# Half of one input load issued from GpSimd's queue instead of SP's

## Chip, cores and metric

The kernel runs on one core of a Trainium2 chip. The metric is the device time of one execution in microseconds (us); before the change it is 413.87 us, the median of 3 runs (413.44 to 415.31).

## What is computed

The input x has 2048 tokens of 448 features. A gate mixes two branches. Branch a is attention with 16 heads of 28 features, in which each token looks at itself and 7 earlier tokens, 2 apart. Branch b is an MLP with 1792 hidden features, biases and a squared ReLU. Cut to what matters:

```
g = sigmoid((x * gate_w).sum(-1, keepdims=True))
q, k, v = split(x @ wqkv)                      # 448 -> 3 x 448
idx = pos[:, None] - 2 * arange(8)             # masked where negative
a = softmax_w(q . k[idx] * 28 ** -0.5) . v[idx] @ wo
b = square(relu(x @ w1 + b1)) @ w2 + b2
out = g * a + (1 - g) * b
```

## The kernel before

**Numbers.** All matrix products keep nearly full float32 accuracy by splitting. Each operand is held as a rounded part (h, for high) and a rest (l, for low), and each product is three matmuls: h by h, h by l, l by h. ScalarE makes the high part by a copy into the rounded type, VectorE the low part by a subtraction.

**Tiles.** The 2048 tokens are cut into four row tiles of 512 tokens (`CH`), numbered c = 0 to 3. The 448 features, over which the first products sum, are cut into K tiles of 128, 128, 128 and 64 rows (k = 0 to 3). The host hands x over transposed, as `xT[c, row, k, token]`, and the weights as `wqkv[b, row, k, column]` with b = 0, 1, 2 for q, k and v.

**Stages.** First the q, k and v products of the four row tiles, beginning with row tile 0 in `qkv_first` (L246); then the MLP on TensorE (`h_first`, `o_part` and so on), beside which GpSimd and VectorE compute the attention (L329 to L346), and at the end the output projection with `wo`. The order of the instructions is written out by hand: `advance` (L471) adds up costs of the matmuls issued so far and emits the other engines' steps when they fall due. Each engine works through its own instructions in the order in which the program emits them.

**The start, where the change is.** Before any data is there, TensorE runs 13 matmuls on zeros (L625). The loads for row tile 0 are issued in the loop at L630, all from SP: for each k the q weights of K tile k (L632, 225 KB; for k = 3 in two parts, L635), and then K tile k of row tile 0 into `rx` (L637), whose name in the profile is xraw. For k = 0 this second load comes in two halves of 256 tokens, 128 KB each; for k = 1 to 3 it is one load of 256 KB. Behind them SP issues the loads of the weights of k and v (L642, L645) and of row tile 1 (`x_load`, L558).

The splits follow in the loop at L647, for k = 0, 1, 2: ScalarE rounds the weights (L648, `wqh`), then the two halves of x (L655), except that the very first half is rounded by VectorE (L653); VectorE subtracts (L656 for the weights, L658 for the halves of x). The last K tile is split at L659 and L660 through `split_full` (L114).

`qkv_first` then takes the K tiles in order. For each k it computes tokens 0 to 255 (output tiles 0 and 1) and then tokens 256 to 511 (output tiles 2 and 3), six matmuls each, at L255:

```
for k in range(3):
    for two in ((0, 1), (2, 3)):
        for j, prods in enumerate(zip(*(full(x, q[i], i, 0, (k,)) for i in two))):
            for acc, a, w in prods:
                nc.tensor.matmul(acc.pt[:, :D], a, w, start=k == j == 0, stop=False)
```

So the second half of K tile 0 is needed by the seventh matmul, and K tile 1 by the thirteenth. The last 64 rows of K, and all of k and v, follow through `side_by_side` (L178, matmul at L186).

GpSimd's instructions up to there are memsets: four constants of the launch, `mask` (L106, L108) and `halo0` (L162). Its next work in program order is the first attention product (L331). Before the change it issues no DMA.

Of the kernel before, what the change touches and what calls it, by code (L numbers as in the profile page):

```python
# [22 lines left out]
CH = 512  # L23
# [34 lines left out]
def gated_mix_kernel(ctx: ExitStack, tc: tile.TileContext, xT, wqkv, w1, w2, wo, b1, b2, out):  # L58
    nc = tc.nc
# [432 lines left out]
    def raw_tile(name):  # L492
        return rawp.tile([P, 4, 512], F32, tag="raw", name=name)
# [135 lines left out]
    rx = raw_tile("xraw0")  # L629
    for k in range(4):  # L630
        if k < 3:
            nc.sync.dma_start(raws[0][:, k, :NQ], wqkv[0, :, k])  # L632
        else:
            for b, rows in ((0, slice(0, 64)), (1, slice(64, P))):
                nc.sync.dma_start(raws[0][rows, k, :NQ], wqkv[b, rows, k])  # L635
        for cols in ((slice(0, 256), slice(256, CH)) if k == 0 else (slice(0, CH),)):
            nc.sync.dma_start(rx[:, k, cols], xT[0, :, k, cols])  # L637

    for b, tag in ((1, "k"), (2, "v")):
        raw = attp.tile([P, 3, D], F32, tag=tag, name=f"wqraw{b}")  # L640
# [569 lines left out]
```

## Time and profile before

| | |
|---|---|
| median of 3 runs | 413.87 us (413.44 to 415.31) |
| profiled execution, its own time | 413.75 us |
| its span (first to last instruction) | 412.0 us |
| DVE (VectorE) busy | 270.5 us, 66% |
| ACT (ScalarE) busy | 210.5 us, 51% |
| POOL (GpSimd) busy | 268.5 us, 65% |
| granted TensorE clock | 1.0 |
| DMA through SP's queue | 73.23 MB; none from another engine's queue |

PE is TensorE, PEld its weight loads, which overlap the matmuls; SPq is SP's queue of DMA issues and POOLq the steps of GpSimd's queue that count as no busy time. A row of the timeline gives start, duration, engine, line, operation, the tiles written and read, their shapes, how many instructions are merged, and in brackets the idle time of the engine ahead of it and what ended it. A row of the waits gives the total in us, how often, and the longest. In the view by stretches each engine has its busy time with the number of its instructions, in the order PE, PEld, DVE, ACT, POOL; behind them stand the granted clock, the busy share of the 16 DMA engines, and GB/s.

### The profile page before, as it was taken

What the parts mean: (1) busy time and instruction counts of PE and PEld (TensorE: products, weight loads), DVE (VectorE), ACT (ScalarE), POOL (GpSimd) and SP (SyncE); (2) the same over time, 40 slices, a digit from 0 to 9 for tenths busy, and PEclk for the clock granted to TensorE, in tenths of its full rate; (3) what the DMA queues carried; (4) which work ended last, traced back from release to release, by engine and by line L of the source; (5) the groups of instructions that cost most, each with busy time, mean ns of one, the idle gap of its engine ahead of it and who ended that gap; (6) DMA issues with size and microseconds to landing.
All of it is one profiled execution on the core that took longest, in us unless ns stands there. A gap on an engine that the chain in (4) does not pass through costs nothing.

```text
span 412.0 us, 9325 instructions
## 1 busy us (share of the span) xinstructions
PE 407.2 (99%) x3835; PEld 371.7 (90%) x3835; DVE 270.5 (66%) x430; ACT 210.5 (51%) x461; POOL 268.5 (65%) x167
## 2 busy tenths in 40 slices
PE   8999999999999999999999999999999999999996
PEld 7999999999999999888888888988898888888996
DVE  4690845287767766787656798879576677882354
ACT  4642647387765555444565535444653254356640
POOL 0000000966989999989989899999899977940000
PEclk9999999999999999999999999999999999999999
DMA  7999899988272325554103649765146530168304
GB/s 215 378 343 324 246 373 277 366 276 302 91 258 82 128 64 196 209 185 152 50 38 113 215 157 270 196 163 141 31 151 196 220 130 2 45 166 147 93 0 181
DMA packets 66331, 73.83 MB, mean 179 GB/s; under 512 B 33072, under 2 KB 59248, under 8 KB 65904
## 3 DMA queue, kind: packets, MB, share of 16 engines
q1 hardware_dynamic: 66288, 73.23, 55.4%
q8 instruction: 30, 0.49, 0.5%
q14 instruction: 13, 0.11, 0.1%
HBM read 45.74 MB, written 28.28 MB: 180 GB/s over the span
## 4 chain that ended last, share of the span: by engine, by line
PE 97%; DMA 1%; SPq 0%; DVE 0%; ACT 0%; issue 0%
PE b L186 33%; PE h L186 32%; PE qkv L186 23%; PE a L186 7%; PE qkv L255 1%; DMA xraw<-xT 1%; PE a L984 1%; PE last L984 0%; SPq L637 0%; SPq L632 0%; DVE bt L863 0%; ACT x L655 0%; PE last L976 0%; PE a L976 0%
## 5 line engine op out<-in xcount | busy, mean ns | idle before, releaser
L331 POOL TENSOR_TENSOR qk<-q,k 128x896 f32<-128x896 f32 x64 | 135.2, 2148 | 83.8 <-DMA k<-k_d 77.1
L338 POOL TENSOR_TENSOR av<-lg,v 128x896 f32<-128x896 f32 x64 | 119.4, 1965 | 6.3 <-DVE lg L332 5.8
L612 DVE TENSOR_TENSOR h<-h,h 128x512 fp32r<-128x512 f32 x56 | 38.4, 688 | 66.3 <-ACT h L615 66.0
L186 PE MATMUL qkv<-wqh,x 64*128 64x448 f32 x528 | 78.6, 359 | 0.0
L186 PE MATMUL b<-w2ah,h 64*128 64x448 f32 x448 | 67.2, 359 | 0.0
L332 DVE TENSOR_REDUCE lg<-qk 128x32 f32<-128x896 f32 x64 | 66.9, 1074 | 0.0
L186 PE MATMUL b<-w2bh,h 64*128 64x448 f32 x448 | 66.8, 360 | 0.0
L346 DVE TENSOR_REDUCE o<-av 128x112 f32<-128x896 f32 x64 | 66.4, 1070 | 0.1
L613 ACT ACTIVATE h<-h,b1z 128x512 f32<-128x512 f32 x56 | 36.7, 655 | 43.6 <-PE h L186 43.6
L186 PEld LDWEIGHTS qkv<-wqh,x 64*128 64x128 f32 x528 | 50.7, 184 | 2.7
L186 PE MATMUL qkv<-wql,x 64*128 64x448 f32 x264 | 48.8, 359 | 0.0
L186 PEld LDWEIGHTS b<-w2bh,h 64*128 64x128 f32 x448 | 42.8, 184 | 3.3 <-ACT h L564 0.3
L186 PEld LDWEIGHTS b<-w2ah,h 64*128 64x128 f32 x448 | 43.1, 184 | 2.9
L186 PE MATMUL b<-w2al,h 64*128 64x448 f32 x224 | 41.2, 358 | 0.0
L186 PE MATMUL b<-w2bl,h 64*128 64x448 f32 x224 | 41.1, 358 | 0.0
L205 ACT ACTIVATE st<-qkv 128x448 f32<-128x448 f32 x48 | 23.4, 540 | 32.5 <-PE qkv L186 28.6
L614 ACT ACTIVATE h<-h 128x512 fp32r<-128x512 f32 x56 | 33.5, 598 | 1.7
L615 ACT ACTIVATE h<-h 128x512 f32<-128x512 f32 x56 | 33.3, 594 | 0.0
L186 PE MATMUL h<-x,w1h 64*128 64x512 f32 x168 | 29.6, 386 | 0.0
L564 ACT ACTIVATE h<-h 128x4 fp32r<-128x4 f32 (+1 forms) x35 | 7.2, 207 | 43.6 <-PE b L186 43.4
L186 PE MATMUL h<-x0b,w1h 64*128 64x512 f32 x168 | 28.1, 386 | 0.0
L186 PE MATMUL h<-x1b,w1h 64*128 64x512 f32 x168 | 28.1, 386 | 0.0
(150 smaller groups left out, 694.2 us busy)
## 6 DMA issues: line engine op xcount, KB each, us to landing
k<-k_d SPq DMA_DIRECT2D x8, 840.0 KB, 5.5
v<-v_d SPq DMA_DIRECT2D x8, 840.0 KB, 4.5
x_d<-x SPq DMA_DIRECT2D x11, 512.0 KB, 7.3
q_d<-st SPq DMA_DIRECT2D x8, 448.0 KB, 5.6
k_d<-st SPq DMA_DIRECT2D x8, 448.0 KB, 6.6
v_d<-st SPq DMA_DIRECT2D x8, 448.0 KB, 6.5
w1raw<-w SPq DMA_DIRECT2D x4, 896.0 KB, 9.8
q<-q_d SPq DMA_DIRECT2D x8, 448.0 KB, 3.7
```

What stands on the lines that cost most here:

```text
L186: nc.tensor.matmul(acc.pt[:, :acc.n], a[rows], w[rows], start=acc.todo == acc.all, stop=acc.todo == 1)
L205: nc.scalar.activation(st[:, :, t % 2], pt[:, :D].rearrange("p (g c) -> p g c", g=G), AF.Copy)
L255: nc.tensor.matmul(acc.pt[:, :D], a, w, start=k == j == 0, stop=False)
L331: nc.gpsimd.tensor_mul(pr, q[:, s:s + 1].to_broadcast([P, W, C]), k[:, s:s + W])
L332: pending.append(lambda: nc.vector.tensor_reduce(lg[:, s], pr.rearrange("p w (h d) -> p w h d", h=HG), axis=AX.X, op=ALU.add))
L338: nc.gpsimd.tensor_mul(pr.rearrange("p (h d) w -> p w h d", h=HG), lg[:, s][:, :, :, None].to_broadcast([P, W, HG, DH]), v[:, s:s + W].rea ...
L346: nc.vector.tensor_reduce(o[:, g * C:(g + 1) * C], pr, axis=AX.X, op=ALU.add)
L564: nc.scalar.activation(ap, f32(ap), AF.Copy)
L612: nc.vector.tensor_sub(hl, pt, f32(hh))
L613: ops += [lambda pt=pt, r=r: nc.scalar.activation(pt, pt, AF.Relu, bias=b1t[:, f + r:f + r + 1]), lambda pt=pt, hh=hh: nc.scalar.activatio ...
L614: lambda pt=pt, hh=hh: nc.scalar.activation(hh, pt, AF.Square),
L615: lambda pt=pt, r=r, low=low: (nc.scalar.activation(pt, pt, AF.Square), at(delays[r], low))]
```

## The change

The load of tokens 256 to 511 of K tile 0 of row tile 0 is issued by GpSimd instead of SP. Its place in the program, its source, its destination and its size are the same, and so are all other loads; for k = 1 to 3 the code is only written differently.

```
         else:
             for b, rows in ((0, slice(0, 64)), (1, slice(64, P))):
                 nc.sync.dma_start(raws[0][rows, k, :NQ], wqkv[b, rows, k])
-        for cols in ((slice(0, 256), slice(256, CH)) if k == 0 else (slice(0, CH),)):
-            nc.sync.dma_start(rx[:, k, cols], xT[0, :, k, cols])
+        if k == 0:
+            nc.sync.dma_start(rx[:, 0, 0:256], xT[0, :, 0, 0:256])
+            nc.gpsimd.dma_start(rx[:, 0, 256:CH], xT[0, :, 0, 256:CH])
+        else:
+            nc.sync.dma_start(rx[:, k], xT[0, :, k])
```

## The prediction

> **What bounds the kernel now.** I read the page's busy table and its chain first, to learn which engine sets the end, and then the chain in order of time for the first 14 us, because the moved transfer is issued there.
>
> ```profile
> PE 407.2 (99%) x3835; PEld 371.7 (90%) x3835; DVE 270.5 (66%) x430; ACT 210.5 (51%) x461; POOL 268.5 (65%) x167
> ...
> 1.66 0.43 SPq L637
> 2.09 0.04 issue
> 2.13 0.43 SPq L632
> 2.56 0.04 issue
> 2.60 4.56 DMA xraw<-xT
> 7.16 0.02 issue
> 7.18 0.43 ACT x L655
> 7.61 0.04 issue
> 7.66 5.08 PE qkv L255 x24
> 12.74 1.41 PE qkv L186 x11
> ```
>
> TensorE is busy for 407.2 of 412.0 us. Only what shifts its whole stream counts, and the chain shows where that can happen: back from the end it runs through TensorE to 7.66 us, and there it leaves TensorE for ScalarE's copy of x, for the landing at 7.16 us of a DMA into xraw issued at 2.60 us, and for SP's issues ahead of it. That DMA is the load of K tile 1 of the first row tile (call it x1; x0a and x0b are the two halves of K tile 0, wq1 the weights of K tile 1, x2 and wq2 the next). x0b is the row at 1.66 us: SP spends 0.43 us on it and 0.04 us before the next issue.
>
> The waits of TensorE over the whole span say how much there is to win.
>
> ```profile
> PE warm L625 <- DVE b1z L623: 1.2, 1, 1.2
> PE qkv L255 <- ACT x L655: 0.3, 1, 0.3
> ```
>
> The 1.2 us are the start of the program and are not touched. The other wait is for x0b. The ends of matmuls are modelled, so I take these gaps from the starts instead:
>
> ```profile
> 5.43 0.37 PE L255 MATMUL qkv<-wqh,x 128*128 128x448 f32 x1
> ...
> 6.11 0.67 PE L255 MATMUL qkv<-wqh,x 128*128 128x448 f32 x2 [0.31 <-ACT x L655]
> ...
> 7.02 0.56 PE L255 MATMUL qkv<-wqh,x 128*128 128x448 f32 x2
> ```
>
> Two matmuls that together take 0.56 us, of 0.36 each, start 0.20 us apart. The last of the first six starts at 5.43, so the next could start at 5.63; it starts at 6.11, 0.48 us late, for x0b. The last of the second six starts at 7.22, so K tile 1 could start at 7.42; it starts at 7.66, 0.24 us late, for x1. Behind the first gap the two matmuls take 0.67 us where 0.56 is usual, 0.11 for the restart. So the stage holds 0.48 + 0.24 + 2 x 0.11 = 0.94 us at most that earlier data could give back.
>
> **The change part by part.** *SP loses one issue.* The row at 1.66 us goes, with the 0.04 us behind it: wq1, x1, wq2, x2 and all later loads of SP are issued 0.47 us earlier, x1 at 2.13. What does x1's landing gain? At least nothing if the DMA engines are the limit, since the same bytes run on them; at most 0.47 us if issuing is. The DMA columns (the last two: busy share, GB/s) of one-microsecond stretches decide:
>
> ```profile
> 3.00:4.00 1.00, 1.00 (x7) 1.00 (x5) 0.24 (x1) 0.58 (x1) 0.00 (x0) 1.00 0.61 123
> 4.00:5.00 1.00, 1.00 (x5) 0.63 (x5) 1.00 (x3) 0.00 (x1) 0.00 (x0) 1.00 0.83 230
> 5.00:6.00 1.00, 0.80 (x4) 0.39 (x3) 0.00 (x0) 0.35 (x1) 0.00 (x0) 1.00 1.02 342
> 6.00:7.00 1.00, 0.89 (x4) 0.85 (x5) 0.55 (x2) 0.64 (x2) 0.00 (x0) 1.00 1.00 305
> ```
>
> From 5 us on the engines are full; from 3 to 5 us they are not: 0.39 + 0.17 = 0.56 us of their time is unused, although x0b, wq1 and x1 are all issued by 3.03 us. x0b is 128 KB (131 thousand bytes), at 342 GB/s 0.38 us of full engines, so it fits into the hole. If it fills the hole while SP's queue goes straight on to wq1, what follows moves up by about that. I take **0.4 us** for x1, between 0 and 0.47, and keep both ends.
>
> *GpSimd gains one issue.* Its engine rows around the place:
>
> ```profile
> 1.21 0.18 POOL L162 MEMSET halo<- 56x112 f32 x1
> 72.12 12.59 POOL L331 TENSOR_TENSOR qk<-q,k 128x896 f32<-128x896 f32 x6 [70.73 <-DMA k<-k_d]
> ```
>
> In its order the DMA comes behind the memset of halo0, which ends at 1.39 us, and ahead of L331 at 72.12 us, which waits for another DMA. So it is issued 0.27 us before SP issues it now, waits for nothing (its buffer is new), and has 70 us in which nothing is queued behind it. GpSimd's own time for it is free here, at whatever price below those 70 us; without that cover it would delay the attention products.
>
> *The landing of x0b.* No DMA of this trace goes through GpSimd's queue, so its time to land has to be bounded. These rows give SP's loads of this stage by the engine that waited for them:
>
> ```profile
> 1.20 0.89 SPq L637 DMA_DIRECT2D xraw<-xT  x2
> ...
> 3.76 0.29 DVE L653 CAST x<-xraw 128x256 fp32r<-128x256 f32 x1 [2.62 <-DMA xraw<-xT]
> ...
> 5.64 0.42 ACT L655 ACTIVATE x<-xraw 128x256 fp32r<-128x256 f32 x1 [1.64 <-DMA xraw<-xT]
> 6.26 0.58 ACT L648 ACTIVATE wqh<-wqraw 128x448 fp32r<-128x448 f32 x1 [0.20 <-DMA wqraw<-wqkv]
> ...
> 9.25 0.73 ACT L655 ACTIVATE x<-xraw 128x256 fp32r<-128x256 f32 x2 [0.85 <-DMA xraw<-xT]
> ...
> w1raw<-w SPq DMA_DIRECT2D x4, 896.0 KB, 9.8
> ```
>
> x0a, of the same shape, lands 3.76 - 1.20 = 2.56 us after its issue, x0b itself now 5.64 - 1.66 = 3.98 us after. From 1.39 us that makes 3.95 to 5.37 us. The far end is the load of w1, seven times as large, with 9.8 us: 11.19 us. I take the nearest rows, the transfer's own two: x0b lands **before 5.4 us**, that is, no later than now.
>
> How late may it land? TensorE starts on x0b 6.11 - 5.64 = 0.47 us after the landing and needs 7.42 - 6.11 = 1.31 us for its six matmuls, so K tile 1 starts no earlier than landing + 1.78. ScalarE, which takes x0b, wq1 and half of x1 in this order, needs 0.42 + 0.58 + 0.43 = 1.43 us from the landing, which is less. With x1 0.4 us earlier, K tile 1 can start at 7.26, so up to a landing at 5.48 us nothing is lost; at 5.88 us (now's 7.66) the change is worth nothing; each further microsecond costs one.
>
> The Trainium skill, "DMA: Bandwidth & Descriptors", section "Issuing engines are not separate DMA queues", says that issuing from several engines saves only the sequencer's time for the issue, since all run on the same 16 engines; the 0.47 us of the row above is that time, and by the rule alone the sum would be 0.47 us. The same page, section "Anatomy of one DMA", puts a transfer from GpSimd at about 2.0 us plus its bytes over 436 GB/s; an estimate by that page is a landing at 3.7 us, earlier than my bound, and no run so far shows it.
>
> *What is late next.* With K tile 1 at 7.26, its twelve matmuls bring K tile 2 to 10.17 - 0.4 = 9.77 us (10.17 is the third start of the row below). x2's first copy ends at 9.25 + 0.42 = 9.67 us even if x2 lands no earlier, so it is just in time. The last 64 rows of K start at 12.27 instead of 12.67; their operand from ScalarE is complete at 10.94 + 0.61 = 11.55 us.
>
> ```profile
> 9.77 0.96 PE L255 MATMUL qkv<-wqh,x 128*128 128x448 f32 x4
> ...
> 10.94 0.61 ACT L115 ACTIVATE x<-xraw 128x512 fp32r<-128x512 f32 x1
> ...
> 12.67 0.48 PE L186 MATMUL qkv<-w7h,x 64*128 64x448 f32 x2
> ```
>
> Behind it TensorE has no wait at all by the table above, so I let the 0.4 us run through to the end.
>
> **Sum.** -0.4 (x1 earlier) + 0 (x0b lands in time) + 0 (GpSimd's issue, hidden) = -0.4 us. The profiled execution took 413.75 us with a span of 412.0; the 1.75 us around it stay. It would be 413.35; the median of the runs shown is 0.12 higher, 413.87, and on that basis the forecast is **413.5 us**.
>
> **The rivals.**
>
> *A, hidden anyway (413.9).* x1's landing is set by the DMA engines, which are full from 5 us to its landing, and x0b's packets now run among wq1's and x1's. Then the earlier issue buys nothing. For it: the shares 1.02 and 1.00 above. Against it: the unused 0.56 us between 3 and 5.
>
> *B, slower: GpSimd's transfer lands late.* One mechanism: the transfer from this queue takes longer than 5.88 - 1.39 = 4.49 us. ScalarE works in order, so wq1 and x1 wait behind it, and TensorE's whole stream shifts. With 5.7 us, what x2 takes now (9.25 - 3.55, SP's issue, the row below), it lands at 7.09, K tile 1 starts at 8.87, 1.21 us late: 415.1. With 9.8 us it lands at 11.19, K tile 1 at 12.97, 5.31 us late: 419.2. For it: no row shows this queue, and this row shows that GpSimd has something else to do at that time:
>
> ```profile
> 3.55 0.43 SPq L637 DMA_DIRECT2D xraw<-xT  x1
> ...
> L331 POOLq MODIFY_POOL_CONFIG  x2: 1/1/1, 1.3 to 1.4; - x2
> ```
>
> Its queue changes a configuration for L331 at 1.3 to 1.4 us, just where the DMA goes. Against it: that step belongs to L331, which stands behind the DMA in program order, and a landing this late would be nearly twice x0a's. The Trainium skill, "GPSIMD Engine Reference", section "Instruction dispatch", says that the first call after such a step also pays a load of code of about 6 us. Were the DMA to stand behind that, an estimate by this page is a landing at 1.4 + 6 + 2.3 = 9.7 us and a time of 417.7 us; here it would hold only if the order of the two were the other way, and no row shows it.
>
> *C, both waits go (412.9).* x0b lands well before 5 us and x1 moves up by more than SP's issue, as its bytes no longer queue behind x0b's: all 0.94 us come back, 412.9. For it: the hole. Against it: x1 would have to land at about 6.3 us, 0.4 us beyond what its earlier issue explains.
>
> **How the numbers follow.** About 0.5% (2.1 us) is what a measurement of this kernel can tell from no change. Forecast, 0.2 to 0.47 us faster: 0.57. A: 0.16. C: 0.06. B: 0.19, of it 0.09 with landings up to 8 us (to 415.9) and 0.10 beyond. All but this last part lie within 0.5%, and no mechanism here gives 2.1 us, since the stage holds 0.94; I leave 0.02 for that. So faster 0.02, same 0.88, slower 0.10. The range goes from 412.9 (C) to 415.1 (B with x2's time to land), and leaves out the late part of B and a little more.
>
> **What would show it.** In the changed profile: SP's issue of wq1 at about 1.66 instead of 2.13 and of x1 at 2.13; a DMA issue on GpSimd at about 1.4; ScalarE's first row of L655 before 5.64; x1's copy at about 6.8 instead of 7.18; K tile 1 at about 7.26; more than 123 GB/s between 3 and 4 us. Wrong it would be if ScalarE's first L655 starts after 5.9 us (B, and then TensorE's wait at L255 grows by the same amount), if x1's copy stays at 7.18 (A), or if a wait of TensorE appears behind 7.66 that is not in the table above.

## The result, and the profile after

The changed kernel takes 415.08 us, the median of 20 runs (414.43 to 415.56); the kernel before takes 413.73 in the runs beside it, also 20. The ratio is 1.0027, with an interval of 1.0019 to 1.0035: by it about 1.1 us slower (0.8 to 1.4), by the medians 1.35, where 0.4 faster was forecast. It lies at the upper end of the range and within the 0.5% that the prediction called "same", but the whole interval is on the slower side. The profiled execution took 415.04 us with a span of 413.3, 1.29 us more than the profiled one of before.

The chain in order of time, of after, where it differs (start, length, what):

```profile
1.66 0.43 SPq L632
2.09 0.04 issue
2.14 6.23 DMA xraw<-xT
8.37 0.02 issue
8.39 0.42 ACT x L658
8.81 0.04 issue
8.86 5.08 PE qkv L255 x24
13.94 0.40 PE qkv L186
```

The path is that of before: SP's issues, x1's landing, ScalarE's copy, TensorE. The row at 1.66 is now wq1's issue, x1 is issued at 2.14 instead of 2.60, and lands at 8.37 instead of 7.16: a load that starts 0.46 us earlier ends 1.21 us later. K tile 1 starts at 8.86 instead of 7.66, 1.20 us late, which is nearly all of the 1.3 by which the span grew.

ScalarE's rows show what it waited for:

```profile
6.07 0.42 ACT L658 ACTIVATE x<-xraw 128x256 fp32r<-128x256 f32 x1 [2.10 <-DMA xraw<-xT]
6.66 0.58 ACT L651 ACTIVATE wqh<-wqraw 128x448 fp32r<-128x448 f32 x1 [0.18 <-DMA wqraw<-wqkv]
8.39 0.72 ACT L658 ACTIVATE x<-xraw 128x256 fp32r<-128x256 f32 x2 [1.15 <-DMA xraw<-xT]
```

x0b is copied at 6.07 us, 0.43 later than before, and wq1 at 6.66 (before 6.26, though it was issued 0.47 earlier). Then ScalarE stands idle for 1.15 us for x1 alone. So x0b is late, but it isn't what holds K tile 1. TensorE's starts give the two prices:

```profile
5.25 0.56 PE L255 MATMUL qkv<-wqh,x 128*128 128x448 f32 x2
6.53 0.68 PE L255 MATMUL qkv<-wqh,x 128*128 128x448 f32 x2 [0.72 <-ACT x L658]
...
7.45 0.57 PE L255 MATMUL qkv<-wqh,x 128*128 128x448 f32 x2
8.86 0.68 PE L255 MATMUL qkv<-wqh,x 128*128 128x448 f32 x2 [0.84 <-ACT x L658]
```

With 0.20 us from start to start, the six matmuls of x0b end such that K tile 1 could start at 7.45 + 0.40 = 7.85. That is 0.19 later than before's 7.66, and it is x0b's whole price. The other 1.01 us, to 8.86, are x1's.

GpSimd's rows show the moved transfer:

```profile
1.21 0.18 POOL L162 MEMSET halo<- 56x112 f32 x1
1.48 0.70 POOL L638 DMA_DIRECT2D xraw<-xT  x1
```

The list of DMA issues gives its time to land:

```profile
xraw<-xT POOLq DMA_DIRECT2D x1, 128.0 KB, 4.6
```

It goes right behind the memset, as the prediction said, and takes GpSimd 0.70 us. It lands 4.6 us after its issue, at about 6.05.

The one-microsecond stretches of after (the last two columns are the DMA engines' busy share and GB/s):

```profile
3.00:4.00 1.00, 1.00 (x7) 1.00 (x5) 0.30 (x2) 0.58 (x1) 0.00 (x0) 1.00 0.78 154
4.00:5.00 1.00, 1.00 (x5) 0.87 (x5) 0.96 (x2) 0.00 (x0) 0.00 (x0) 1.00 0.76 213
5.00:6.00 1.00, 0.82 (x5) 0.42 (x3) 0.00 (x0) 0.00 (x0) 0.00 (x0) 1.00 1.03 281
6.00:7.00 1.00, 0.47 (x2) 0.45 (x3) 0.42 (x1) 0.76 (x2) 0.00 (x0) 1.00 0.96 269
```

The hole from 3 to 5 us was hardly used: 367 thousand bytes moved in it, 353 before. From 5 to 7 us 550 thousand moved where before moved 647, with the engines as busy (1.03 and 0.96; before 1.02 and 1.00). The engines didn't stand still; they moved less in the same busy time. How much of x1's lateness this explains is worked out further down.

### The profile page after: what moved, and what is told of

It is laid out like the page before. It is cut to its first block, busy times and chain, and to the rows that moved or that the text cites. A ratio compares the mean times of both kernels' runs of the same rounds, so it can differ in the third digit from the quotient of the medians.

```text
span 413.3 us, 9326 instructions
## 1 busy us (share of the span) xinstructions
PE 407.1 (99%) x3835; PEld 364.8 (88%) x3835; DVE 270.6 (65%) x430; ACT 210.3 (51%) x461; POOL 269.1 (65%) x168
## 4 chain that ended last, share of the span: by engine, by line
PE 97%; DMA 2%; SPq 0%; DVE 0%; ACT 0%; issue 0%
PE b L186 33%; PE h L186 32%; PE qkv L186 23%; PE a L186 7%; DMA xraw<-xT 2%; PE qkv L255 1%; PE a L987 1%; PE last L987 0%; SPq L632 0%; DVE bt L866 0%; ACT x L658 0%; SPq L637 0%; PE last L979 0%; PE a L979 0%
## 5 line engine op out<-in xcount | busy, mean ns | idle before, releaser
L331 POOL TENSOR_TENSOR qk<-q,k 128x896 f32<-128x896 f32 x64 | 135.1, 2140 | 84.0 <-DMA k<-k_d 76.2
L186 PE MATMUL b<-w2ah,h 64*128 64x448 f32 x448 | 66.3, 359 | 0.0
L186 PEld LDWEIGHTS qkv<-wqh,x 64*128 64x128 f32 x528 | 49.5, 184 | 3.5
L186 PE MATMUL qkv<-wql,x 64*128 64x448 f32 x264 | 47.6, 358 | 0.0
L186 PEld LDWEIGHTS b<-w2ah,h 64*128 64x128 f32 x448 | 41.9, 184 | 3.7
L186 PE MATMUL h<-x,w1h 64*128 64x512 f32 x168 | 28.1, 386 | 0.0
```

Source lines behind the costliest of these rows:

```text
L186: nc.tensor.matmul(acc.pt[:, :acc.n], a[rows], w[rows], start=acc.todo == acc.all, stop=acc.todo == 1)
L331: nc.gpsimd.tensor_mul(pr, q[:, s:s + 1].to_broadcast([P, W, C]), k[:, s:s + W])
```

## The experiments

There are eighteen kernels, e1 to e18. Each has its ratio to the kernel before in runs on the same chip. The table gives what the sections behind it come back to: the times of issue of x0b, wq1 and x1, and the start of K tile 1 on TensorE where TensorE waited there, both from the profiled execution. Those of e11 and e17 were the slowest of their ten, with a late x0a, so nothing rests on their landings (in e11's, x1 was copied at 7.54 us already); those of e5, e15 and e18, their slowest too, are read with that in mind. "No wait" says that x1 was there when TensorE came to K tile 1, not that K tile 1 was early: in e6, for one, the first matmuls start 0.37 us apart, where before and after have 0.20 from about 5 us on, and K tile 1 starts at about 7.98. Times of x1's issue before 2.5 us are in bold.

| kernel | x0b issued | wq1 | x1 | K tile 1 starts | ratio (interval) |
|---|---|---|---|---|---|
| before | SP 1.66 | 2.13 | 2.60 | 7.66 | 1 |
| after | GpSimd 1.48 | 1.66 | **2.14** | 8.86 | 1.0027 (1.0019 to 1.0035) |
| e1 | SP 1.66 | 2.13 | 2.60 | no wait | 0.9997 (0.9988 to 1.0007) |
| e2 | GpSimd | 1.66 | **2.14** | 8.96 | 1.0025 (1.0015 to 1.0036) |
| e3 | SP | 2.12 | 2.60 | x1 copied at 7.45 | 0.9999 (0.9988 to 1.0010) |
| e4 | ScalarE | 1.66 | **2.13** | no wait, start of all late | 1.0033 (1.0011 to 1.0055) |
| e5 | SP 2.60 | 1.65 | **2.13** | x0b's part at 8.39 | 1.0066 (1.0047 to 1.0084) |
| e6 | GpSimd | 2.13 | 2.61 | no wait | 1.0004 (0.9994 to 1.0013) |
| e7 | SP | 2.13 | 2.61 | 7.42 | 1.0009 (0.9999 to 1.0018) |
| e8 | SP | 2.14 | 2.61 | 8.13 | 1.0029 (1.0017 to 1.0040) |
| e9 | GpSimd 1.49 | 2.28 | 2.65 | no wait | 0.9999 (0.9989 to 1.0008) |
| e10 | GpSimd 1.49 | 1.66 | 2.61 | no wait | 1.0004 (0.9991 to 1.0017) |
| e11 | GpSimd | 1.66 | **2.14** | not read | 1.0022 (1.0012 to 1.0032) |
| e12 | SP 2.13 | 1.66 | 2.60 | no wait | 1.0006 (0.9996 to 1.0016) |
| e13 | GpSimd | 1.66 | 2.59 | no wait | 1.0007 (0.9993 to 1.0022) |
| e14 | GpSimd | 1.66 | **2.42** | 8.46 | 1.0020 (1.0010 to 1.0031) |
| e15 | GpSimd | 2.13 | **1.66** | 9.65 | 1.0034 (1.0022 to 1.0046) |
| e16 | SP 1.66 | 2.60 | **2.13** | 8.98 | 1.0029 (1.0019 to 1.0039) |
| e17 | GpSimd | 1.66 | **2.13** and 2.6, by columns | not read | 1.0004 (0.9993 to 1.0016) |
| e18 | GpSimd | 1.66 | **2.14** and 2.75, by rows | 8.78 | 1.0013 (1.0003 to 1.0023) |

The expectations number the theories as they came up, and each says what its theories mean.

### Is it GpSimd's change of configuration? (e1 to e3)

The first suspect was rival B's second mechanism: the step that changes GpSimd's configuration went from 1.3 us in before to 2.2 in after, among the loads. A small copy on GpSimd, put far behind the loads, moves the step away; e1 does this to before, e2 to after.

```
             zu.rearrange("p (t b r) -> p t b r", t=4, b=4), axis=AX.X, op=ALU.add)
+        if c == 0:
+            nc.gpsimd.tensor_copy(b1z[0:1, 14:15], zpart[0:1, 0:1])
```

> The kernel before, plus one copy of one element on GpSimd that reads a result of VectorE made at about 24 us; it stands ahead of L331, so GpSimd's MODIFY_POOL_CONFIG moves from 1.3 us to about 24 us. Theory 1 (the step sets off a load that slows the DMA engines for some microseconds, and the change made it later by 0.9 us): without it in the first 14 us the hole in the DMA rate at 3 to 5 us closes and x1 lands about 1 us earlier, at about 6.2 us; span some 0.5 to 0.9 us shorter, about 413.0 us. Theory 2 (GpSimd's transfer takes turns with SP's on the 16 engines and holds them up): no such transfer here, so 413.7 us and x1 still at 7.16 us.

> The changed kernel with the same copy: MODIFY_POOL_CONFIG moves from 2.2 us to about 24 us, x0b stays on GpSimd. Theory 1: x0b and x1 land early, x1 by 6.7 us or before, time 412.8 to 413.3 us. Theory 2: as the changed kernel, x1 at about 8.4 us, 415.1 us.

The rows of e1's line L331 show that the step moved:

```profile
L331 POOLq MODIFY_POOL_CONFIG  x2: 1/1/1, 24.3 to 24.4; - x2
```

e1: 413.77 us, no change. e2, with the step at 25.4: 414.95, and in its chain x1's landing is as late as in after:

```profile
2.14 6.33 DMA xraw<-xT
8.47 0.02 issue
8.49 0.42 ACT x L658
8.92 0.04 issue
8.96 5.08 PE qkv L255 x24
```

e3 goes the other way: in before, a memset keeps GpSimd busy, which brings the step to 2.3 us, where after has it.

```
     nc.gpsimd.memset(halo0, 0.0)
+    nc.gpsimd.memset(w1h[:, 0, :1152].bitcast(F32), 0.0)
```

> The kernel before, plus one memset of about 0.8 us on GpSimd behind that of halo0, so that MODIFY_POOL_CONFIG comes at about 2.1 us as in the changed kernel, while all loads stay on SP. Theory 1: x1 lands about 1 us later than before, some 414.7 us, most of the change's loss without the change. Theory 2: 413.7 us.

413.82 us, no change. With the step at 1.3, 2.3 or 24 us before shows no loss, and with it at 25 us after keeps its own. That theory (1 in the expectations) falls.

### Is it GpSimd's queue, or what SP does with the place that came free? (e4 to e8)

e4 leaves SP as in after and lets ScalarE's queue issue x0b:

```
-            nc.gpsimd.dma_start(rx[:, 0, 256:CH], xT[0, :, 0, 256:CH])
+            nc.scalar.dma_start(rx[:, 0, 256:CH], xT[0, :, 0, 256:CH])
```

> x0b issued from ScalarE's queue instead of GpSimd's, so SP is free of it and GpSimd does what it did before, with MODIFY_POOL_CONFIG at 1.3 us. Theory 1: no loss; x1 lands by about 7.0 us, 413.3 to 413.8 us. Theory 2, if any second queue does it: x1 later than 7.5 us and about 415 us; if only GpSimd's queue does it, as theory 1.

Ratio 1.0033, with a wide interval (1.0011 to 1.0055). Slower without GpSimd, though in the profiled execution at another place: x0b is issued at 0.74 us, ahead of all others, x0a lands at 5.13, and TensorE starts at 5.59. That execution took 414.18 us, where most of the others took 415.7 to 416.7, so its trace doesn't show the loss. This run speaks against GpSimd's queue as the only cause, but tells little of x1.

e5 has no second queue at all: before, with x0b issued behind x1.

```
-        for cols in ((slice(0, 256), slice(256, CH)) if k == 0 else (slice(0, CH),)):
-            nc.sync.dma_start(rx[:, k, cols], xT[0, :, k, cols])
+        nc.sync.dma_start(rx[:, k, :256 if k == 0 else CH], xT[0, :, k, :256 if k == 0 else CH])
+        if k == 1:
+            nc.sync.dma_start(rx[:, 0, 256:CH], xT[0, :, 0, 256:CH])
```

> All loads on SP; x0b is issued behind x1 instead of behind x0a, so wq1 and x1 are issued 0.47 us earlier, as in the changed kernel, and no other engine issues anything. What tells is x1's landing (issue to landing in the view by tile). Theory 2 (GpSimd's transfer beside SP's holds SP's up): x1 lands at about 6.7 us, 4.6 us after its issue. Theory 3 (with x0b out of the way the later loads of SP crowd each other, and x1's slowest engine falls behind whatever queue carries x0b): x1 lands at 8 us or later. The time is no verdict: x0b itself comes later, and TensorE's second six matmuls wait for it; about 414 us by theory 2, 415 us by theory 3.

416.37 us, the median of four. x0b, issued at 2.60, lands at 7.89, and everything waits for it, as the chain shows:

```profile
2.60 5.29 DMA xraw<-xT
```

The same five loads left SP at the same five times as in before, in another order, and the DMA engines moved 236 GB/s from 5 to 7 us (323 in before). x1's own landing, on which the expectation turned, can't be read, since nothing waited for it. Nor are the whole 2.6 us the load's. Behind TensorE's wait of 2.38 us its granted clock was 0.62 from 8 to 9 us and 0.50 from 9 to 11, where before has 1.00, and the matmuls started 0.37 us apart instead of 0.20. The two executions with a mean clock of 0.995 took 417.0 and 417.15 us, the two with 0.998 and 0.999 took 415.59 and 415.74.

e6 is after with SP's old times: the 7 KB load of b1, which needs no particular place, takes x0b's old one.

```
             nc.gpsimd.dma_start(rx[:, 0, 256:CH], xT[0, :, 0, 256:CH])
+            nc.sync.dma_start(b1t, b1)
...
-        nc.sync.dma_start(b1t, b1)
```

> The changed kernel, with the small load of b1 (7 KB) put into SP's queue where x0b was, so that all of SP's other loads are issued at the times of the kernel before; x0b stays on GpSimd. Theory 2: x1 still late, about 8.2 us or later, 415 us. Theory 3: x1 back at about 7.2 us, 413.8 us.

413.90 us: the loss is gone, and x0b still goes through GpSimd's queue. ScalarE's first copy of x1 waits for no DMA:

```profile
7.06 0.73 ACT L659 ACTIVATE x<-xraw 128x256 fp32r<-128x256 f32 x2
```

e7 is before, with b1's load alone on GpSimd:

```
         for cols in ((slice(0, 256), slice(256, CH)) if k == 0 else (slice(0, CH),)):
             nc.sync.dma_start(rx[:, k, cols], xT[0, :, k, cols])
+            if k == 0 and cols.start:
+                nc.gpsimd.dma_start(b1t, b1)
...
-        nc.sync.dma_start(b1t, b1)
```

> The kernel before, with the load of b1 (7 KB) issued by GpSimd at the place where the change issues x0b; all of x stays on SP. If the mere use of GpSimd's queue slows SP's loads: x1 at 8 us, 415 us. If the bytes of GpSimd's transfer do it (theory 2) or the order on SP (theory 3): as before, x1 at 7.2 us, 413.8 us.

413.98 us, no change that could be told. e8 is before, with 128 KB more ahead of x1: the second half of K tile 3 through GpSimd.

```
-        for cols in ((slice(0, 256), slice(256, CH)) if k == 0 else (slice(0, CH),)):
-            nc.sync.dma_start(rx[:, k, cols], xT[0, :, k, cols])
+        for cols in ((slice(0, 256), slice(256, CH)) if k in (0, 3) else (slice(0, CH),)):
+            if k < 3 or not cols.start:
+                nc.sync.dma_start(rx[:, k, cols], xT[0, :, k, cols])
+            if k == 0 and cols.start:
+                nc.gpsimd.dma_start(rx[:, 3, cols], xT[0, :, 3, cols])
```

> The kernel before, with the second half of K tile 3 (128 KB, the same shape as x0b) issued by GpSimd at the place where the change issues x0b; SP issues everything up to x2 at the times of the kernel before. It brings 128 KB ahead of x1, worth 0.38 us at 342 GB/s. Theory 2: x1 later by far more than that, at 8 us or later, about 415 us. Theory 3: x1 later by at most 0.4 us, at 7.2 to 7.6 us, at most 414.2 us.

414.58 us, 1.0029: as much as after loses, with x1 issued at before's time. In the profiled execution (414.22, the fastest of its seven) x1's copy moves to 7.66, by 0.48 us, about what 131 thousand bytes take at 298 to 342 GB/s (0.38 to 0.44); the rest of the ratio isn't explained by these rows. So more bytes beside x1 cost time too, and e8 fits neither expectation: theory 2 had about 415 with x1 at 8 us or later, theory 3 at most 414.2. But GpSimd's queue as such costs nothing that could be told (e7), and neither does x0b in it (e6), so theory 2 isn't what slows after. What e6 shares with before, and after doesn't, is when SP issues wq1 and x1.

### Which of SP's issues must not come early? (e9 to e16)

e9 is after; SP's issue of wq1 waits for two memsets on VectorE (which has nothing else to do then), so wq1 goes at 2.28 and x1 at 2.65.

```
+            if k == 1:
+                for _ in range(2):
+                    nc.vector.memset(raws[0][:, 1, :NQ], 0.0)
             nc.sync.dma_start(raws[0][:, k, :NQ], wqkv[0, :, k])
```

> The changed kernel, with two memsets of VectorE (idle then) on the place that wq1 is loaded to, so that SP's issue of wq1 waits until about 2.1 us, and x1 and all behind it keep the times of the kernel before; no small load is added. Theory 3a (it is the earlier time of wq1 and x1 behind x0a that costs): as with the small load, x1 at 7.0 to 7.4 us, 413.9 us. Theory 3b (the small load in SP's queue helps by being there): still late, x1 after 8 us, 415 us.

413.82 us: a delay removes the loss. SP's rows, and then ScalarE's:

```profile
2.28 0.33 SPq L635 DMA_DIRECT2D wqraw<-wqkv  x1
2.65 0.43 SPq L643 DMA_DIRECT2D xraw<-xT  x1
```

```profile
6.89 0.72 ACT L661 ACTIVATE x<-xraw 128x256 fp32r<-128x256 f32 x2
```

x1 leaves 0.51 us later than in after and is copied 1.50 us earlier.

e10 and e11 divide the two loads: b1's small load stands behind wq1 (x1 at its old time), or behind x1 (wq2 at its old time).

```
             nc.sync.dma_start(raws[0][:, k, :NQ], wqkv[0, :, k])
+            if k == 1:
+                nc.sync.dma_start(b1t, b1)
...
-        nc.sync.dma_start(b1t, b1)
```

> The changed kernel with the small load of b1 on SP between wq1 and x1: wq1 is issued early at 1.66 us, x1 and all behind it at the times of the kernel before. If wq1's early issue costs: x1 at 8 us or later, about 415 us. If x1's early issue costs: x1 at about 7.2 us, 413.9 us.

```
             nc.sync.dma_start(rx[:, k], xT[0, :, k])
+            if k == 1:
+                nc.sync.dma_start(b1t, b1)
...
-        nc.sync.dma_start(b1t, b1)
```

> The changed kernel with the small load of b1 on SP behind x1: wq1 and x1 issued early, at 1.66 and 2.13 us, wq2 and all behind it at the times of the kernel before. If the early issue of wq1 or of x1 costs: x1 at 8 us or later, about 415 us. If it is the crowd of the later loads: x1 at about 6.7 us, 413.5 us.

e10: 413.86 us. An early wq1 alone does no harm that could be told. e11: 414.92 us. The loss is there with wq2 at its old time, so it isn't wq2's.

e12 has all on SP, wq1 ahead of x0b:

```
             nc.sync.dma_start(raws[0][:, k, :NQ], wqkv[0, :, k])
+            if k == 1:
+                nc.sync.dma_start(rx[:, 0, 256:CH], xT[0, :, 0, 256:CH])
...
-        for cols in ((slice(0, 256), slice(256, CH)) if k == 0 else (slice(0, CH),)):
+        for cols in ((slice(0, 256),) if k == 0 else (slice(0, CH),)):
```

> All loads on SP, none on GpSimd; only x0b and wq1 change places: wq1 at 1.66 us, x0b at 2.13, x1 at 2.60 as before. If wq1's early issue behind x0a costs whatever queue carries x0b: x1 at 8 us or later and about 415 us. If it costs only beside a transfer of GpSimd: x1 at about 7.2 us; x0b 0.5 us later than before, at about 6.1 us, so about 414.0 us.

414.05 us, no loss that can be told. Against e5, which differs only in that x0b and x1 are exchanged (2.13 and 2.60), that is 0.0060 of the time less, 2.5 us, of which a part is e5's lower clock.

e13 tests the suspicion directly: after, with nothing delayed but x1 (and what follows it), by three memsets on VectorE; e14 has two, for a smaller delay.

```
+            if k == 1:
+                nc.vector.memset(rx[:, 1, :448], 0.0)
+                nc.vector.memset(rx[:, 1, :448], 0.0)
+                nc.vector.memset(rx[:, 1, :176], 0.0)
             nc.sync.dma_start(rx[:, k], xT[0, :, k])
```

> After, with three VectorE memsets on x1's part of the buffer, so that SP's issue of x1 waits for them and goes at about 2.6 us; wq1 stays early (1.66), x0b on GpSimd, no small load. If x1's issue time alone decides (theory 3): time as before, 413.8 (ratio 1.000 within 0.001), x1's first copy at 6.9 to 7.4. If it is the bytes that are queued by about 2.2 us, whichever load they belong to (theory 4): the same, since x1's 256 KB are not yet queued then. If the time of the small load of the run after_small_behind_wq1 mattered, or wq2's issue: about 415.

```
+            if k == 1:
+                nc.vector.memset(rx[:, 1, :512], 0.0)
+                nc.vector.memset(rx[:, 1, :512], 0.0)
             nc.sync.dma_start(rx[:, k], xT[0, :, k])
```

> The same with two memsets, x1 issued at about 2.40 us, half way between after's 2.14 and before's 2.60. Theories 3 and 4 name no threshold: a loss that grows with the lead gives about 414.4 (1.001 to 1.002); a threshold below 2.40 gives 413.8, one above it 415.

e13: 414.08 us, ratio 1.0007 (0.9993 to 1.0022). By the time alone a part of the loss could be left, but x1, issued at 2.59, is copied at 7.02:

```profile
7.02 0.72 ACT L662 ACTIVATE x<-xraw 128x256 fp32r<-128x256 f32 x2 [0.31 <-DMA xraw<-xT]
```

e14: 414.64 us, 1.0020. Issued at 2.42, x1 lands at 7.96, by its chain:

```profile
2.42 5.55 DMA xraw<-xT
7.96 0.02 issue
7.99 0.42 ACT x L661
8.41 0.04 issue
8.46 5.07 PE qkv L255 x24
```

So 2.14 us gives a landing at 8.37, 2.42 one at 7.96, and 2.59 one at 7.00: a lead of 0.17 us over e13 already costs 0.96 at the landing, in one execution each.

e15 and e16 exchange wq1 and x1, in after and in before:

```
+            if k == 1:
+                nc.sync.dma_start(rx[:, k], xT[0, :, k])
             nc.sync.dma_start(raws[0][:, k, :NQ], wqkv[0, :, k])
...
-        else:
+        elif k > 1:
             nc.sync.dma_start(rx[:, k], xT[0, :, k])
```

> After with wq1 and x1 exchanged in SP's order: x1 issued at 1.66 us, wq1 at 2.14, x0b by GpSimd at 1.49. Theory 3 (x1's issue time): x1's first copy is as late as in after or later (8.4 or more), time 415 or more. Theory 4 (bytes queued by 2.2 us, 970 KB as in after): whichever load is last among them lands late, so x1 is in time but wq1 lands at 8 us or later, and the time is 414.5 to 415.5.

```
+            if k == 1:
+                nc.sync.dma_start(rx[:, k], xT[0, :, k])
             nc.sync.dma_start(raws[0][:, k, :NQ], wqkv[0, :, k])
...
-        for cols in ((slice(0, 256), slice(256, CH)) if k == 0 else (slice(0, CH),)):
+        for cols in ((slice(0, 256), slice(256, CH)) if k == 0 else (slice(0, CH),) if k > 1 else ()):
             nc.sync.dma_start(rx[:, k, cols], xT[0, :, k, cols])
```

> Before with wq1 and x1 exchanged in SP's order, all on SP: x0b at 1.66 us, x1 at 2.13, wq1 at 2.60. Theory 3 (x1's issue time): x1's first copy at 8 us or later, 414.8 or more. Theory 4 (bytes queued by 2.2 us: 741 KB, where the kernels without a loss have 714 and those with a loss 842 to 970): 413.8 to 414.1, wq1 and x1 both landed by 7.4.

e15: 414.91 us. e16: 414.97 us. The late load is now wq1; its rows in the chain of e15, then of e16:

```profile
2.13 6.56 DMA wqraw<-wqkv
...
9.65 4.47 PE qkv L255 x21
```

```profile
2.60 5.42 DMA wqraw<-wqkv
...
8.98 5.09 PE qkv L255 x24
```

e16 decides between the theories: GpSimd issues nothing, the amount queued by 2.2 us is near that of kernels without a loss (by the loads' sizes 737 KB; 706 in e12 and e13, 713 in e10), and yet the time is that of after. Theory 4 falls. Theory 3 holds for the time, but not in the words in which it was put: x1 need not be the load that lands late. It was x0b in e5 and wq1 in e15 and e16; with x1 early, either x1 itself or a load issued behind it is late.

### What about x1? (e17 and e18)

Both are after with x1 in two transfers of 128 KB, the first at 2.13 or 2.14 us. e17 cuts by columns (rows of 1024 bytes, the form of x0b), e18 by rows of the tile (still 2048 bytes each).

```
-            nc.sync.dma_start(rx[:, k], xT[0, :, k])
+            for cols in ((slice(0, 256), slice(256, CH)) if k == 1 else (slice(0, CH),)):
+                nc.sync.dma_start(rx[:, k, cols], xT[0, :, k, cols])
```

> After with x1 in two transfers by SP, each 128 KB with rows of 1024 bytes: the first half of its columns at 2.14 us, the second at 2.61; wq2 and what follows is issued as in before. So half of x1's bytes are early. If early bytes of x1 slow what is beside them whatever their form (theory 3): half the loss or more, 414.3 to 415, second copy of x1 at 8 us or later. If the form matters (rows of 2048 bytes, theory 5): no loss, 413.8, x1's first copy at 6.6 to 7.3, since x0b, of this very form, does no harm at 2.13 us.

```
-            nc.sync.dma_start(rx[:, k], xT[0, :, k])
+            for rows in ((slice(0, 64), slice(64, P)) if k == 1 else (slice(0, P),)):
+                nc.sync.dma_start(rx[rows, k], xT[0, rows, k])
```

> After with x1 in two transfers by SP, partitions 0 to 63 at 2.14 us and 64 to 127 at 2.61: 128 KB each as in the run beside it, but rows of 2048 bytes. Theory 3 (early bytes of x1): 414.3 to 415, as in the run beside it. Theory 5 (rows of 2048 bytes): a loss here, 414.3 to 415, and none there. If neither loses, it is the amount of x1's bytes that are early that decides, and half of it is below the point.

e17: 413.88 us, 1.0004 (0.9993 to 1.0016): no loss with half of x1 early. e18: 414.31 us, 1.0013 (1.0003 to 1.0023): about half of it. Its chain (execution of 414.88 us):

```profile
2.75 5.47 DMA xraw<-xT
8.22 0.02 issue
8.24 0.02 ACTq L659
8.26 0.05 issue
8.31 0.42 ACT x L659
8.73 0.04 issue
8.78 5.08 PE qkv L255 x24
```

That fits theory 5 of the expectations, that early rows of 2048 bytes are what hurts, but the two intervals overlap, and e18's second half was issued at 2.75 and not 2.61, so it isn't shown. No kernel here is measurably faster than before: the best are e1, e3 and e9, at 0.9997 to 0.9999.

## Why the prediction was wrong

**The bound.** Right. The chain runs through x1's landing to K tile 1, and what K tile 1 lost, 1.20 us, came out at the end.

**"I take 0.4 us for x1".** This is the step that failed, and with it the argument "if it fills the hole while SP's queue goes straight on to wq1, what follows moves up by about that". The issue moved up by 0.46 us, as predicted; the landing moved back by 1.21, and K tile 1 started 1.20 us later instead of 0.4 earlier. I had bounded the gain from below by nothing, "since the same bytes run on them". That supposed that it doesn't matter to x1 when and in which order the loads beside it are issued. e5 contradicts this: the same five loads left SP at the same five times, in another order, and x0b, issued 0.94 us later than in before, landed 2.27 us later. The hole was hardly used either: from 3 to 5 us before moved 353 thousand bytes, after 367.

That SP's earlier issues make the loss is shown by e6 and e9 (all of SP's loads at about before's times: gone), and that it is x1's by e10 and e13 (x1 and what follows it held back: gone) with e11 (only what follows x1 held back: there). e16 has the loss without GpSimd, with wq1 and x1 exchanged; wq1 is issued 0.47 us later there, and lands 1.78 later. An early x1 isn't the only way to such a loss: e8 has it from 128 KB more.

**Why x1 landed late: rate or order?** After moved less, but that is the smaller part. By 7.16 us, x1's landing in before, it had moved 1.25 million bytes and before 1.35; at 323 GB/s this is 0.3 of the 1.21 us. And when x1 did land in after, at 8.37, 1.60 million had moved. So other loads moved more ahead of x1's last bytes than in before, and the sizes of the packets show which. Until 9 us only x1, x2 and x3 (K tile 3) have packets of 2048 bytes, 128 each; x0b through GpSimd's queue makes 32 packets of 4096. A landing comes a little behind its last packet (for x0b 0.32 us in before and 0.49 in e5), so with an allowance I count until 0.5 us ahead of x1's landing, to 6.66 us in before and to 7.87 in after (all packets, and those under a size):

```profile
DMA packets 840, 1.19 MB, mean 179 GB/s; under 512 B 88, under 2 KB 695, under 8 KB 840
```

```profile
DMA packets 902, 1.46 MB, mean 185 GB/s; under 512 B 109, under 2 KB 652, under 8 KB 902
```

In before 840 - 695 = 145 packets of 2048 bytes had started, in after 902 - 652 - 32 = 218. At most 128 of them are x1's. So in after at least 90 packets of x2 and x3, which were issued 0.94 us and more behind x1, were served ahead of x1's last ones; in before it is at least 17, and in e13, counted alike, 19. By this count x1 was late mainly because loads behind it came ahead of its end.

The Trainium skill, "DMA: Bandwidth & Descriptors", section "Issuing engines are not separate DMA queues", by which a saved issue is worth the sequencer's time and no more, agrees with e6 and e7 as far as issuing from GpSimd changed no time that could be told. No run here gained those 0.47 us, and in after the saved issue cost 1.2, which that rule alone doesn't give.

**x0b's landing.** Wrong by a little. I took its own former row and said before 5.4 us; it landed at 6.05, 4.6 us after its issue, outside the bounds of 3.95 to 5.37 that I called near and 0.17 past the limit of 5.88. Its price by the rows is 0.19 us at K tile 1, and x1's own lateness covers even that. With x1 at its old time it lands a little earlier and costs nothing that could be told (copied at 5.87 in e6, 5.73 in e9).

The Trainium skill, "DMA: Bandwidth & Descriptors", section "Anatomy of one DMA", gave the estimate of a landing at 3.7 us; the 6.05 measured is 2.3 later, among other transfers.

**GpSimd's issue.** Right: it comes behind the memset, takes GpSimd 0.70 us, lies 70 us ahead of its next work, and costs nothing. **What is late next** was never reached.

**The rivals.** A had the right objection (the engines are full from 5 us on), but would have ended at no change. B gave the measured time, 415.1 us, by luck: with a landing at 7.09 of x0b. Its sign, a first copy after 5.9 us, did appear (6.07), but x0b landed at 6.05, and the load that made K tile 1 wait was x1, on SP. Moving the configuration step (e1 to e3) changed nothing that could be told, and in after it ran behind the DMA, at 2.2 us. C's condition, a landing of x1 at 6.3, was missed by 2 us.

**The chances.** 0.10 stood for slower by over 0.5% and 0.88 for the band in which the result lies; but 0.63 of it was on the side of a gain. What was missing is a rival in which the earlier issue itself does harm. And the 0.5% taken as the least that can be told from no change was too coarse: with 20 runs of each kernel the interval around 0.27% leaves out zero.

**What stays open.** Why loads behind an early x1 come ahead of its end, and why less moves. The traces don't tell which of the 16 DMA engines took a packet, so an engine that falls behind, as e5's expectation has it, fits but isn't shown, nor is a port. The hole from 3 to 5 us is in before and in after, but not in all kernels: in e4, which issues x0b ahead of all others, 254 GB/s moved from 3 to 4 us. In one execution each, x1 at 2.42 us was late and at 2.59 was not; and with its rows cut in two no harm could be told.

## What to carry to other kernels

Where several loads are in flight at once, an earlier issue is not a gain that can only be zero at worst; look for a loss as well, and ask not only how many bytes move but whose packets come last. When an issue moves to another queue, the first suspect is what moves up in the old queue: hold its times with a small load or a wait, as in e6, e9 and e13, and the two effects come apart at once. A rival that names the right time isn't thereby the right cause; the wait row of the engine says which load was late.

## What the runs showed of the hardware

- x1 (256 KB, rows of 2048 bytes) issued at 2.14, 2.42 and 2.59 us landed at 8.37, 7.96 and 7.00: later issue, earlier landing.
- In after the DMA engines were as busy from 5 to 7 us as before (1.03 and 0.96 against 1.02 and 1.00), and moved 15% less.
- Loads of one queue didn't end in the order of issue: in after at least 90 packets of x2 and x3 had started 0.5 us before x1 landed, though SP issued x1 0.94 us ahead of x2 (at least 17 in before).
- 128 KB through GpSimd's queue took 4.6 us to land and 0.70 us of GpSimd's row, where SP's queue needed 3.98 and 0.43 for the same transfer in before.
- The step that changes GpSimd's configuration changed nothing measurable at 1.3, 2.3 or 24 us (e1, e3).
- Behind a wait of 2.38 us of TensorE, the granted clock in e5's profiled execution was 0.50 from 9 to 11 us, and its matmuls started 0.37 us apart instead of 0.20.
